# Attention and squared-ReLU feed-forward on one core: the order of issue planned from reads and writes

## The chip, the cores and the metric

The kernel runs on one core of one Trainium2 chip. The metric is the device time of one execution in microseconds (us). Three runs of the kernel before gave 759.31, 759.48 and 760.11 us; their median, 759.48 us, is the time before.

## The reference

There are B = 8 batches, H = 8 heads, S = 512 tokens, 32 state rows per head and D = 64. Both attentions below are computed, their results are joined, and every one of the 8 x (512 + 32) = 4608 rows goes through a feed-forward of width 2048.

```python
def _attn_ref(x, state):                        # x 8x8x512x64, state 8x8x32x64
    scores = scale * np.matmul(x, state.transpose(0, 1, 3, 2))
    a = softmax(scores)                         # over the 32 state rows
    xread = np.matmul(a, state)
    scores2 = scale * np.matmul(state, x.transpose(0, 1, 3, 2))
    a2 = softmax(scores2)                       # over the 512 tokens
    sread = np.matmul(a2, x)
    return np.concatenate([xread, sread], axis=2)

def _moe_ref(x, w_in, w_out):                   # w_in 512x2048, w_out 2048x512
    r = np.maximum(x @ w_in, 0.0)
    return (r * r) @ w_out
```

The weights arrive as 64-bit floats (looked at as pairs of 32-bit words) and are turned into 32-bit floats on the chip.

## The kernel before, in words

**Precision.** Products that need 32-bit accuracy at a high rate are made of three: a value is split into a rounded part `hi` and a remainder `lo` (`split`, L97: ScalarE copies, VectorE or GpSimd subtracts), and hi*hi, lo*hi and hi*lo are added up in PSUM.

**The main loop.** The token rows never form `xread`. Instead z = state x w_in is computed once per batch group, and the hidden layer of a batch is softmax x z. One *unit* is one batch b and one block `fc` of 128 hidden columns (16 units per batch, 128 in all). In `mlp` (L342) `up` makes 6 matmuls of 128x512 into `ph` (L353), then ScalarE takes the ReLU `r` (L355), VectorE multiplies `ph` by `r` (L359; for the first 10 units ScalarE squares, L357), and `split` gives `g_hi` and `g_lo` (L98, L99). `down` makes 12 matmuls of 128x512 into four accumulators `po` (L379), 8 of them with `g_hi` and 4 with `g_lo`. The up of a unit stands ahead of the down of earlier ones. The state rows of all batches (256) go through a last round of 16 units at the end, with 12 up matmuls of 128x256 and 6 down matmuls each.

**z.** `z_state` loads the states of four batches, `z_part` (L142) multiplies them by w_in: four matmuls over 64 rows, in two pairs (`pz0` on the upper 64 rows, `pz1` on the lower; L151), into two tiles, which ScalarE copies (L157) and a DMA writes to memory (`zd`). `z_fetch` (L179) reads a batch's share back in four DMAs (`z_raw`) and splits it. The group of batches 0 to 3 and that of 4 to 7 have 16 such parts each. For batch 0 the first three pairs of blocks are computed directly instead (`z_direct`, L165: `pzd`).

**The attention of a batch** is in two halves g of 256 channels. `scores` (L241) multiplies x by the states (`pst`, L257; from batch 2 on in split form, `pq`, L247). VectorE turns the result in blocks of 32 (`q`, L262), takes maxima and sums, subtracts and scales (L274 to L284), turns back (`at`, L286), and `split` gives `a_hi` and `a_lo`, without which no unit of the batch can start. In the first batches the subtraction and the scaling run on GpSimd (`pool_early`). `turn` and `read` (L297, L312: `pt`, `pr`) make the other attention two batches later.

**The weights.** Each of 16 tiles of w_in (256 columns of half the rows) and 16 of w_out is loaded (512 KB), converted by one ScalarE and three VectorE instructions (`singles`, L101: L104, L105, L108, L112), and w_out is also split, its `lo` on GpSimd (L412). All of it happens during batch 0. Four raw buffers hold tiles that are loaded and not yet converted.

**What sets the order.** The source lists the first steps by hand (L499) and spreads the rest over slots between ups and downs by due times (`Ahead`, L436). The tile framework then reorders all instructions by a timeline simulation of its own (`schedule_with_timeline_sim=True`, L639). Every engine takes its instructions in the order that results; nearly all loads are issued from one queue, SP's.

Of the kernel before, what the change touches and what calls it, by code (L numbers as in the profile page):

```python
# [9 lines left out]
F32 = mybir.dt.float32  # L10
# [6 lines left out]

@with_exitstack
def memory_attention_then_relu2_ffn(
# [10 lines left out]

# [10 lines left out]
    NCC = DM // P  # L52
    NFC = DF // P
# [27 lines left out]

    ident = const.tile([P, P], F32, name="ident")
    make_identity(nc, ident)

    wo = [None] * NFCH
    sp_hl = const.tile([P, NG, 2, 2, 2 * N], F32R, name="sp_hl")
    nc.gpsimd.memset(sp_hl.bitcast(F32), 0.0)
    sp_f = const.tile([P, NG, 2, P + D], F32, name="sp_f")
    nc.gpsimd.memset(sp_f, 0.0)
    sr = [const.tile([P, C], F32, name=f"sr{i}") for i in range(NGB)]  # L90
    wi = const.tile([P, NFCH, NCC, FW], F32, name="wi")
    zd, st = {}, {}
    for G in range(NGB):
        for k in range(NFCH):
            zd[G, k] = dr.tile([P, NG, HG, FW], F32, name=f"zd_{G}_{k}")

    def split(hi, lo, src, eng_lo):  # L97
        nc.scalar.copy(out=hi, in_=src)  # L98
        eng_lo.tensor_sub(out=lo, in0=src, in1=hi.bitcast(F32))  # L99

    def singles(out_f, words):  # L101
        low, high = words[..., 0], words[..., 1]
        bits = out_f.bitcast(I32)
        nc.scalar.activation(out_f, high.bitcast(F32), AF.Abs, scale=GUARD)  # L104
        nc.vector.tensor_scalar(  # L105
            out=bits, in0=bits, scalar1=3, scalar2=None, op0=ALU.logical_shift_left
        )
        nc.vector.scalar_tensor_tensor(  # L108
            out=bits, in0=high, scalar=-0x80000000, in1=bits,
            op0=ALU.bitwise_and, op1=ALU.bitwise_or,  # L110
        )
        nc.vector.scalar_tensor_tensor(  # L112
            out=bits, in0=low, scalar=29, in1=bits,
            op0=ALU.logical_shift_right, op1=ALU.bitwise_or,
        )
# [12 lines left out]
    def z_load(k, g):
        box = {}
        nq = NCC // NG  # L130

        def load():
            raw = sb.tile([P, nq, FW, 2], I32, name="w_raw", tag="raw", bufs=RAW)
            nc.sync.dma_start(out=raw.rearrange("p c f w -> p (c f w)"), in_=w_in[k * NG + g])
            box["raw"] = raw

        def convert():
            singles(wi[:, k, g * nq:(g + 1) * nq, :], box.pop("raw"))

        return load, convert  # L140

    def z_part(G, k, g):  # L142
        nq = NCC // NG

        def product():
            pz = [ps_x.tile([P, nq, FW], F32, name=f"pz{i}", tag="px") for i in range(2)]
            for q in range(nq):
                for i in range(2):
                    own = slice(i * D, (i + 1) * D)
                    cc = g * nq + q  # L150
                    nc.tensor.matmul(  # L151
                        pz[i][:, q, :], lhsT=st[G][own, cc, :], rhs=wi[own, k, cc, :],
                        start=True, stop=True,
                    )
            stage = sb.tile([P, nq, 2, FW], F32, name="z_stage", bufs=2)
            for i in range(2):
                nc.scalar.copy(out=stage[:, :, i, :], in_=pz[i])  # L157
            nc.scalar.dma_start(
                out=zd[G, k][:, g].rearrange("p h f -> p (h f)"),
                in_=stage.rearrange("p q i f -> p (q i f)"),  # L160
            )

        return product

    def z_direct(k, pool, tag):  # L165
        pz = pool.tile([P, NG, FW], F32, name="pzd", tag=tag)
        nq = NCC // NG
        for g in range(NG):
            for q in range(nq):
                nc.tensor.matmul(  # L170
                    pz[:, g, :], lhsT=sp_f[:, g].rearrange("p q n -> p (q n)")[:, q * P:(q + 1) * P],
                    rhs=wi[:, k, g * nq + q, :], start=q == 0, stop=q == nq - 1,
                )
        hi = sb.tile([P, NG, FW], F32R, name="z_hi", bufs=2)
        lo = sb.tile([P, NG, FW], F32R, name="z_lo", bufs=2)
        split(hi, lo, pz, nc.vector)
        return hi, lo

    def z_fetch(b, k):  # L179
        hi = sb.tile([P, NG, FW], F32R, name="z_hi", bufs=2)  # L180
# [4 lines left out]
        for j in range(HG):  # L185
            nc.sync.dma_start(out=raw[j * N:(j + 1) * N], in_=src[:, :, j, :])
# [456 lines left out]
```

## Time and profile before

| what | value |
|---|---|
| time, median of three runs | 759.48 us |
| time of the profiled execution | 758.9 us |
| its span, first to last instruction | 757.1 us |
| TensorE (PE) busy | 720.4 us, 3136 records |
| VectorE (DVE) busy | 437.4 us |
| ScalarE (ACT) busy | 379.7 us |
| GpSimd (POOL) busy | 154.3 us |
| mean granted TensorE clock | 0.96 |

PE busy is the union of modelled, overlapping matmul records; how much work stands in a stretch is seen from the distance of starts, not from it. PEld is the loading of weights. The granted clock is the share of full speed that TensorE was given. A matmul with plain 32-bit operands (`pst`, `pzd`, `pz`) leaves two records, one with split operands leaves one. The span is 1.8 us shorter than the execution's time.

### The profile page before, as it was taken

The page shows a single profiled execution, that of the slowest core. Times are in us where ns is not written, and L with a number is a line of the kernel's source. Part 1 is how long each engine was busy: PE and PEld are TensorE (multiplying, and loading weights), DVE is VectorE, ACT ScalarE, POOL GpSimd, SP SyncE. Part 2 cuts the span into 40 slices and gives each one's busy share as a digit, 9 for nine tenths or more (in the row PEclk, how much of TensorE's full clock was granted, in tenths as well). Part 3 has the DMA queues.
Part 4 walks back from the last instruction along what each step waited for, and adds up shares of the span by engine and source line. Part 5 has one row for each costly group of instructions (what it writes and reads, how often), then busy time and mean ns, then how long its engine had stood idle before and what let it go on. Part 6 is the DMA issues. An engine that isn't in the chain of part 4 may idle for free.

```text
span 757.1 us, 9414 instructions
## 1 busy us (share of the span) xinstructions
PE 720.4 (95%) x3136; PEld 562.1 (74%) x3136; DVE 437.4 (58%) x725; ACT 379.7 (50%) x714; POOL 154.3 (20%) x170
## 2 busy tenths in 40 slices
PE   4899799999999999986999999999999999999997
PEld 2566456778777776755888888888888888888896
DVE  5999952354854333356477487478468534534453
ACT  4477565354654443454465565466446534533443
POOL 1333540022410211023223222223213211100000
PEclk9589879999999999996999999999999999999999
DMA  9588632332123223242121321141213211200101
GB/s 303 199 276 281 239 143 90 111 122 87 58 86 127 102 92 111 99 180 82 45 86 60 118 78 57 57 139 58 62 61 117 80 28 47 66 28 1 57 1 28
DMA packets 49216, 76.90 MB, mean 102 GB/s; under 512 B 6800, under 2 KB 32528, under 8 KB 49168
## 3 DMA queue, kind: packets, MB, share of 16 engines
q1 hardware_dynamic: 44368, 59.27, 24.7%
q10 hardware_dynamic: 4800, 17.04, 5.6%
q8 instruction: 24, 0.39, 0.2%
q14 instruction: 24, 0.20, 0.1%
HBM read 50.59 MB, written 25.69 MB: 101 GB/s over the span
## 4 chain that ended last, share of the span: by engine, by line
PE 83%; DVE 7%; DMA 5%; ACT 2%; issue 1%; POOL 1%; SPq 1%; DVEq 0%; ACTq 0%
PE po L379 48%; PE ph L353 25%; PE pz L151 5%; PE pr L316 2%; DMA wo_raw<-w_out 2%; PE pq L247 1%; DVE wi L108 1%; DMA w_raw<-w_in 1%; DVE wof L108 1%; PE pt L304 1%; DVE wi L112 1%; DVE wof L112 1%; DMA xn_raw<-xn 1%; DVE wof L105 1%; DMA zd<-z_stage 1%
## 5 line engine op out<-in xcount | busy, mean ns | idle before, releaser
L379 PE MATMUL po<-wo_hi,g_hi 128*128 128x512 f32 x544 | 218.0, 401 | 3.2 <-ACT g_hi L98 3.2
L379 PE MATMUL po<-wo_lo,g_hi 128*128 128x512 f32 x544 | 214.9, 395 | 0.0
L359 DVE TENSOR_TENSOR ph<-ph,r 128x512 f32<-128x512 f32 (+1 forms) x134 | 89.1, 665 | 183.8 <-ACT r L355 183.4
L355 ACT ACTIVATE r<-ph 128x512 f32<-128x512 f32 (+1 forms) x144 | 82.7, 575 | 173.7 <-PE ph L353 173.2
L379 PE MATMUL po<-wo_hi,g_lo 128*128 128x512 f32 x544 | 152.1, 393 | 0.0
L99 DVE TENSOR_TENSOR g_lo<-ph,g_hi 128x512 fp32r<-128x512 f32 (+1 forms) x144 | 94.6, 658 | 58.5 <-ACT g_hi L98 34.2
L379 PEld LDWEIGHTS po<-wo_hi,g_hi 128*128 128x128 f32 x544 | 102.9, 189 | 29.7 <-ACT g_hi L98 5.6
L379 PEld LDWEIGHTS po<-wo_lo,g_hi 128*128 128x128 f32 x544 | 102.9, 189 | 23.0 <-issue 1.9
L379 PEld LDWEIGHTS po<-wo_hi,g_lo 128*128 128x128 f32 x544 | 101.0, 188 | 22.3 <-issue 1.0
L98 ACT CAST g_hi<-ph 128x512 fp32r<-128x512 f32 (+1 forms) x144 | 81.2, 564 | 48.5 <-DVE ph L359 36.9
L99 POOL TENSOR_TENSOR xn_hl<-xn_raw,xn_hl 128x512 fp32r<-128x512 f32 x32 | 42.7, 1335 | 230.8 <-ACT xn_hl L98 230.8
L353 PE MATMUL ph<-a_hi,z_hi 128*128 128x512 f32 x256 | 84.1, 410 | 1.2 <-ACT a_hi L98 0.7
L353 PE MATMUL ph<-a_hi,z_lo 128*128 128x512 f32 x256 | 84.6, 408 | 0.0
L353 PE MATMUL ph<-a_lo,z_hi 128*128 128x512 f32 x256 | 82.1, 402 | 0.0
L151 PE MATMUL pz<-wi,st_z 64*128 64x256 f32 x256 | 72.5, 443 | 9.4 <-ACT z_stage L157 5.6
L151 PEld LDWEIGHTS pz<-wi,st_z 64*128 64x128 f32 x256 | 43.1, 207 | 36.3 <-issue 9.8
L99 POOL TENSOR_TENSOR xt_hl<-xt_raw,xt_hl 128x512 fp32r<-128x512 f32 x24 | 31.4, 1309 | 151.9 <-ACT xt_hl L98 121.7
L353 PEld LDWEIGHTS ph<-a_hi,z_lo 128*128 128x128 f32 x256 | 49.5, 194 | 14.1 <-issue 2.6
L353 PEld LDWEIGHTS ph<-a_hi,z_hi 128*128 128x128 f32 x256 | 47.7, 193 | 15.4 <-issue 3.0
L157 ACT COPY z_stage<-pz 128x512 f32<-128x512 f32 x64 | 37.2, 588 | 43.3 <-PE pz L151 42.0
L353 PEld LDWEIGHTS ph<-a_lo,z_hi 128*128 128x128 f32 x256 | 49.5, 194 | 11.4 <-DVE wof L105 0.3
L99 DVE TENSOR_TENSOR z_lo<-z_raw,z_hi 128x512 fp32r<-128x512 f32 x61 | 45.1, 739 | 7.7 <-ACT z_hi L98 7.7
(116 smaller groups left out, 707.0 us busy)
## 6 DMA issues: line engine op xcount, KB each, us to landing
zd<-z_stage ACTq DMA_DIRECT2D x32, 512.0 KB, 2.8
z_raw<-zd SPq DMA_DIRECT2D x244, 64.0 KB, 2.3
xt_raw<-xT SPq DMA_DIRECT2D x16, 512.0 KB, 3.5
w_raw<-w_in SPq DMA_DIRECT2D x16, 512.0 KB, 5.0
wo_raw<-w_out SPq DMA_DIRECT2D x16, 512.0 KB, 4.3
xn_raw<-xn SPq DMA_DIRECT2D x16, 512.0 KB, 3.7
st_z<-stT SPq DMA_DIRECT2D x4, 128.0 KB, 5.9
sp_raw<-stP SPq DMA_DIRECT2D x7, 64.0 KB, 2.6
```

The costliest lines, as they stand in the source:

```text
L98: nc.scalar.copy(out=hi, in_=src)
L99: eng_lo.tensor_sub(out=lo, in0=src, in1=hi.bitcast(F32))
L105: nc.vector.tensor_scalar(out=bits, in0=bits, scalar1=3, scalar2=None, op0=ALU.logical_shift_left)
L108: nc.vector.scalar_tensor_tensor(out=bits, in0=high, scalar=-0x80000000, in1=bits, op0=ALU.bitwise_and, op1=ALU.bitwise_or,)
L112: nc.vector.scalar_tensor_tensor(out=bits, in0=low, scalar=29, in1=bits, op0=ALU.logical_shift_right, op1=ALU.bitwise_or,)
L151: nc.tensor.matmul(pz[i][:, q, :], lhsT=st[G][own, cc, :], rhs=wi[own, k, cc, :], start=True, stop=True,)
L157: nc.scalar.copy(out=stage[:, :, i, :], in_=pz[i])
L316: nc.tensor.matmul(pr[:, q].rearrange("p i c -> p (i c)"), lhsT=my["e"][:, t, q].rearrange("p i n -> p (i n)"), rhs=my["xn"][q][:, t].rear ...
L353: nc.tensor.matmul(ph, lhsT=w, rhs=v, start=i == 0, stop=i == len(todo) - 1)
L355: nc.scalar.activation(r, ph, AF.Relu)
L359: nc.vector.tensor_mul(out=ph, in0=ph, in1=r)
L379: nc.tensor.matmul(po[t], lhsT=g, rhs=w, start=i == 0 and j == 0, stop=i == last and j == 2)
```

## The change

A planner in the source takes the place of the hand-made list, of the slots and of the framework's reordering. Every step becomes an operation with its engines, a cost per engine, what it reads and writes, and sometimes a due time, an earliest time or a chain. `Planner.run` walks through time: at each step it takes the engine that can begin first and on it, of the operations that can begin within 0.02 us, the one due soonest; buffers are taken and given back as it goes. The order in which it picks is the program's order (`manual_schedule`, `schedule_with_timeline_sim=False`).

```diff
+class Planner:
+    RATE = 360.0
+    LAND = 2.2
...
+            t, e, o = best
...
+            o.run(e)
+            end = t + cost
+            if e == "POOL":
+                pool_end = end
+            elif o.both and e == "DVE":
+                end = max(end, pool_end + cost)
...
+def dve(n):
+    return ("DVE", 0.07 + n / 960)
...
+def gps(n):
+    return ("POOL", 0.15 + n / 450)
...
+    START, FIRST, STEP = 18.0, 5.4, 4.4
```

Besides the order, the work itself changes in these places.

**w_in by column tile.** A tile is now 128 columns of all 512 rows, so that one tile is what a unit needs; its size, its DMA and its conversion are as before. `z_direct` works on one block (6 calls of half the width), and `wi` is laid out by block.

```diff
-            np.ascontiguousarray(moe_w_in).view(np.int64).reshape(2, -1, 128, DF // 256, 256)
-            .transpose(3, 0, 2, 1, 4)
-        ).reshape(DF // 256 * 2, 128, -1),
+            np.ascontiguousarray(moe_w_in).view(np.int64).reshape(-1, 128, DF // 128, 128)
+            .transpose(2, 1, 0, 3)
+        ).reshape(DF // 128, 128, -1),
```

**Batch 0's softmax with tokens on partitions.** For batch 0 the scores are also computed turned (`sT`: 8 matmuls of 128x64 per half, with x as the weights), the softmax reads them from PSUM, and TensorE turns the result back (`pa`) in place of VectorE's two transposes. The untransposed product `pst`, which the other attention needs, is made later. Batch 0's subtraction and scaling run on VectorE, and so does the `lo` of w_out; from batch 2 on those of the softmax, with the `lo` of its result, run on GpSimd.

```diff
+            def product_t(e):
+                for t in range(NT):
+                    for q in range(NQ):
+                        nc.tensor.matmul(
+                            flat(sT.t)[:, t * P + q * 2 * N:t * P + (q + 1) * 2 * N],
+                            lhsT=xt.t[:, q, t * P:(t + 1) * P], rhs=sp_f[:, g, q, :2 * N],
+                            start=True, stop=True,
+                        )
...
+            begin=0.0 if b else START + 4.0,
...
-        split(wo[k][0][:, i, :], wo[k][1][:, i, :], wf, nc.gpsimd)
+        split(
+            lambda: wo[k][0][:, i, :], lambda: wo[k][1][:, i, :], lambda: wf.t, DM,
+            [wf], [("wo", 0, fc)], [("wo", 1, fc)],
+        )
```

**Down in pieces.** The 12 down matmuls of a unit are an operation of 8 (with `g_hi`) and one of 4 (with `g_lo`); in a batch's first unit the 8 are four operations of 2, in its last unit there are four of 3, one for each `po`, at the turn from one batch to the next. The four matmuls of a z part are one operation.

**What stands where now.** First, TensorE in the program's first rows. Before, the scores of batch 0 (`pst`) come first, then direct z (`pzd`), and a z part already stands ahead of and between the first unit's up (`ph`):

```order
L257 MATMUL pst<-xt_raw,sp_f 128x512 x4
L170 MATMUL pzd<-wi,sp_f 128x256 x10
L151 MATMUL pz_334<-wi,st_z 128x256 x2
L170 MATMUL pzd<-wi,sp_f 128x256 x2
L151 MATMUL pz_335<-wi,st_z 128x256 x2
L353 MATMUL ph<-a_hi,z_hi 128x512 x3
```

After, the turned scores come first, and only two blocks of direct z and the turning back stand ahead of the first up; `pst` comes behind two units' ups:

```order
L514 MATMUL sT<-sp_f,xt_raw 128x64 x16
L387 MATMUL pzd<-wi,sp_f 128x128 x4
L557 MATMUL pa<-ident,q_157 128x128 x4
L557 MATMUL pa<-ident,q_168 128x128 x4
L387 MATMUL pzd<-wi,sp_f 128x128 x4
L678 MATMUL ph<-a_hi,z_hi 128x512 x2
```

The first up moved ahead of two thirds of the direct z and of all z parts. Second, a z part of the second group on TensorE, in the middle of batch 2. Before, the framework put the pair of `pz0` (`pz_2131`) and that of `pz1` (`pz_2132`) at different places, here with half a down and half an up between:

```order
L151 MATMUL pz_2131<-wi,st_z 128x256 x2
L379 MATMUL po_1948<-wo_lo_574,g_hi 128x512
L379 MATMUL po_1949<-wo_hi_573,g_hi 128x512
L379 MATMUL po_1949<-wo_lo_574,g_hi 128x512
L379 MATMUL po_1946<-wo_hi_573,g_lo 128x512
L379 MATMUL po_1947<-wo_hi_573,g_lo 128x512
L379 MATMUL po_1948<-wo_hi_573,g_lo 128x512
L379 MATMUL po_1949<-wo_hi_573,g_lo 128x512
L353 MATMUL ph<-a_hi,z_hi 128x512 x2
L353 MATMUL ph<-a_hi,z_lo 128x512
L151 MATMUL pz_2132<-wi,st_z 128x256 x2
```

After, in batch 3, the four stand together and alternate between the two tiles, and an up stands between the 8 and the 4 matmuls of a down:

```order
L714 MATMUL po_2745<-wo_lo_87,g_hi 128x512
L678 MATMUL ph<-a_hi,z_hi 128x512 x2
L678 MATMUL ph<-a_hi,z_lo 128x512 x2
L678 MATMUL ph<-a_lo,z_hi 128x512 x2
L714 MATMUL po_2695<-wo_hi_86,g_lo 128x512
L714 MATMUL po_2703<-wo_hi_86,g_lo 128x512
L714 MATMUL po_2710<-wo_hi_86,g_lo 128x512
L714 MATMUL po_2745<-wo_hi_86,g_lo 128x512
L357 MATMUL pz_2912<-wi,st_z 128x256
L357 MATMUL pz_2913<-wi,st_z 128x256
L357 MATMUL pz_2912<-wi,st_z 128x256
L357 MATMUL pz_2913<-wi,st_z 128x256
```

All 32 z parts read like this now, and the up ahead of a unit's down is that of the unit three further on. Third, SP's queue during batch 0, where the loads of weights (`w_raw`, `wo_raw`) and of x (`xn_raw`) share the queue with what reads z back from memory (`z_raw` from `zd_3`, the first that batch 0 needs). Before, it stands behind every load of weights and two loads of x:

```order
L134 DMA w_raw<-w_in 128x1024
L405 DMA wo_raw<-w_out 128x1024 x3
L228 DMA xn_raw<-xn 128x4x256
L405 DMA wo_raw<-w_out 128x1024 x2
L228 DMA xn_raw<-xn 128x4x256
L186 DMA z_raw<-zd_3_87 32x2x256 x4
```

After, three such fetches stand among the loads of weights:

```order
L322 DMA z_raw<-zd_3_103 32x2x256 x4
L322 DMA w_raw<-w_in 128x1024 x2
L322 DMA wo_raw<-w_out 128x1024 x2
L322 DMA w_raw<-w_in 128x1024
L322 DMA z_raw<-zd_4_104 32x2x256 x4
L322 DMA w_raw<-w_in 128x1024
L322 DMA wo_raw<-w_out 128x1024 x2
L322 DMA w_raw<-w_in 128x1024 x2
L322 DMA wo_raw<-w_out 128x1024 x3
L322 DMA z_raw<-zd_5_105 32x2x256 x4
```

The reading back of z for batch 0's fourth pair of blocks (`zd_3`) moved from behind the loads of weights to a place ahead of the last 6 of w_in and 8 of w_out.

More of the change, by code (lines that the diff above doesn't have):

```diff
@@ L80, in memory_attention_then_relu2_ffn, with tile_ @@
     ps_x = ctx.enter_context(tc.tile_pool(name="ps_x", bufs=2, space=bass.MemoryType.PSUM))
+    BUFS = dict(
+        raw=4, xraw=2, x_hl=1, z_stage=2, st_z=1, z_raw=2, z_hi=2, z_lo=2, a_hi=2, a_lo=2,
+        sp_raw=2, st=1, at=1, st_low=1, q1=2, e2=4, s2=4, nm2=2, m1=2, s1=2, e_hl=1, both=1, low=1,
+        r=2, g_hi=2, g_lo=2, os_=3, wof=2, po=4, ph=2, px=2,
+    )
+    plan = Planner()
+    op = plan.op
+    def tile_(shape, dtype, name, tag=None):
+        tag = tag or name
+        pool = {"po": ps_o, "ph": ps_h, "px": ps_x}.get(tag, sb)
+        return Buf(pool, shape, dtype, name, tag, BUFS[tag], hot=tag in ("px", "x_hl"))
@@ L126, in z_state, with z_part, product @@
         st[G] = raw
[L128 to L147, printed above, removed]
+    def z_part(G, k, g, begin=0.0):
+        pz = [tile_([P, NQ, FW], F32, f"pz{i}", "px") for i in range(2)]
+        stage = tile_([P, NQ, 2, FW], F32, "z_stage")
+        def product(e):
+            for q in range(NQ):
@@ L156, in product @@
[L156 to L160, printed above, removed]
-            )
[L163 to L177, printed above, removed]
+        op(("PE", 1.2), product, r=[("wi", k * FPC + i) for i in range(FPC)] + [(st[G], 0), (st[G], 1)], w=pz, begin=begin)
@@ L179, in z_fetch @@
     def z_fetch(b, k):
-        hi = sb.tile([P, NG, FW], F32R, name="z_hi", bufs=2)
-        lo = sb.tile([P, NG, FW], F32R, name="z_lo", bufs=2)
-        raw = sb.tile([P, NG, FW], F32, name="z_raw", bufs=2)
+        raw = tile_([P, NG, FW], F32, "z_raw")
         at = (b % GB) * N
@@ L536, in aux @@
-    def aux():
-        weights.run()
-        reads.run()
-        slot[0] += 1
-    spill = {}
-    for b, fcs in parts:
-        zc = {}
-        while any(w["soft1b"] not in emitted for w in attentions[b][2]):
-            reads.next()
-        def first(fc, b=b, zc=zc):
-            k, i = divmod(fc, FPC)
-            if k not in zc:
-                zc[k] = direct.pop(k) if b == 0 and k < DIRECT else z_fetch(b, k)
-            f = slice(i * P, (i + 1) * P)
-            z_hi, z_lo = zc[k]
-            a_hi, a_lo = a_of[b]
+                        in0=both.t[i * N:(i + 1) * N, q, i * D:(i + 1) * D],
@@ L590, in first @@
[L590 to L603 removed]
+                (w.t[:, cc, :], v.t[:, cc, :])
@@ L605, in rows @@
             at = (t * GB + j) * R + S
-            eng = nc.sync if j % 2 else nc.scalar
-            eng.dma_start(out=out[at:at + N, :], in_=tile_[j * N:(j + 1) * N, :])
-    mlp(NS, range(NFC), first, rows, lambda: None)
+            load(
+                lambda at=at: out[at:at + N, :], lambda os_=os_, j=j: os_.t[j * N:(j + 1) * N, :], 64,
+                r=[os_], w=[("outs", t, j)], due=when[u] + 60, eng="SP" if j % 2 else "ACT", hold=None,
+            )
+    with tc.manual_schedule():
+        plan.run()
```

970 lines of the change are left out of this document (608 added, 362 removed).

## The prediction

> **What bounds the kernel now.** I read the page first, for the shares of the engines and TensorE's clock over time:
>
> ```profile
> PE 720.4 (95%) x3136; PEld 562.1 (74%) x3136; DVE 437.4 (58%) x725; ACT 379.7 (50%) x714; POOL 154.3 (20%) x170
> PEclk9589879999999999996999999999999999999999
> ```
>
> TensorE is the bound, and its clock drops in two places, in the first sixth and in slice 18 (about 340 us). What full speed means is read from the chain of waits in a quiet stretch:
>
> ```profile
> 668.79 2.75 PE po L379 x12
> 671.54 1.37 PE ph L353 x6
> 672.91 2.75 PE po L379 x12
> ```
>
> 18 matmuls of 128x512 take 4.12 us, 0.229 us each, and nothing else stands between. So a stretch loses time where its matmuls, at such prices, don't fill it. Then the windows, cut where the character changes:
>
> ```profile
> 0.00:33.00 33.00, 19.57 (x41) 10.74 (x42) 23.96 (x50) 14.63 (x28) 8.77 (x13) 0.82 0.77 253
> 33.00:61.00 28.00, 26.52 (x85) 18.10 (x86) 26.15 (x41) 20.07 (x37) 9.14 (x6) 0.79 0.80 260
> 61.00:81.00 20.00, 19.00 (x75) 13.27 (x75) 18.20 (x29) 12.75 (x24) 6.56 (x4) 1.00 0.89 295
> 81.00:107.00 26.00, 20.31 (x51) 11.57 (x51) 22.32 (x35) 15.67 (x32) 16.24 (x12) 0.67 0.51 181
> 107.00:161.00 54.00, 53.77 (x231) 39.79 (x228) 16.24 (x24) 23.70 (x43) 1.30 (x1) 1.00 0.31 110
> 161.00:330.00 169.00, 167.44 (x727) 126.98 (x725) 81.07 (x132) 82.31 (x152) 29.53 (x35) 1.00 0.28 96
> 330.00:356.00 26.00, 18.20 (x56) 12.39 (x56) 14.32 (x24) 14.81 (x30) 8.87 (x10) 0.67 0.42 156
> 356.00:705.00 349.00, 348.54 (x1579) 287.11 (x1580) 211.08 (x347) 174.95 (x326) 73.90 (x89) 1.00 0.21 66
> ```
>
> Columns: stretch, length, busy time and records of PE, PEld, DVE, ACT and POOL, granted clock, DMA share, GB/s. From 107 us on TensorE is busy throughout, except at 330 to 356. Up to 107 us only 252 matmul records start; DVE is busy for 90.6 of those 107 us and POOL for 40.7. The kernel is thus three things: a start bound by the conversion of weights and the first softmax, one hole at batch 3, and 570 us of pure TensorE.
>
> **The change, part by part.** *The first unit.* The timeline of the start:
>
> ```profile
> 2.26 1.36 SPq L200 DMA_DIRECT2D sp_f<-stP  x2
> 8.61 6.40 PE L257 MATMUL pst<-xt_raw,sp_f 128*128 128x512 f32 x8 [8.61 <-DMA sp_f<-stP]
> 14.85 1.89 PE L170 MATMUL pzd<-wi,sp_f 128*128 128x256 f32 x8
> 32.81 1.65 PE L353 MATMUL ph<-a_hi,z_hi 128*128 128x512 f32 x3
> ```
>
> TensorE waits for the states until 8.6 and for batch 0's `a_hi` until 32.8. After, the states are issued one load earlier: I take 8 us. No row shows the turned scores, 16 matmuls or 32 records of 64 columns. The nearest from below is `pzd` (0.236 us a record), from above the scores as they are (0.80 us a record of 512): 7.6 to 25.6 us. I take 7.6, since a record four times as narrow as `pzd` can at most be held by its weight load. The first half is then ready at 11.8 us and the second at 15.6. From there DVE's order holds 14 full-width operations and some small ones up to the second `a_lo`. What one costs is in the timeline:
>
> ```profile
> 23.48 0.43 DVE L105 TENSOR_SCALAR wi<-wi 128x512 int32<-128x512 int32 x1
> 23.81 0.69 DVE L112 SCALAR_TENSOR_TENSOR wi<-w_raw,wi 128x512 int32<-128x512 int32 x1
> 24.41 0.69 DVE L108 SCALAR_TENSOR_TENSOR wof<-wo_raw,wof 128x512 int32<-128x512 int32 x1
> 29.30 0.91 DVE L108 SCALAR_TENSOR_TENSOR wof<-wo_raw,wof 128x512 int32<-128x512 int32 x1
> 29.62 1.71 POOL L99 TENSOR_TENSOR wo_lo<-wof,wo_hi 128x512 fp32r<-128x512 f32 x1
> 30.13 1.48 DVE L105 TENSOR_SCALAR wi<-wi 128x512 int32<-128x512 int32 x1
> ```
>
> From start to start 0.33 us for a single-source operation, 0.60 for a two-source one; beside a POOL operation the same single-source one takes 1.48. 14 x 0.60 = 8.4 us of DVE work thus give the first up at 24 us (21 if the turned scores are faster, 28 with hand-overs), against 32.8.
>
> *The rest of batch 0.* After the change DVE's order holds, up to the 16th `g_lo`, 130 two-source operations, 36 single-source ones, 6 of half width and 18 small ones: 130 x 0.60 + 36 x 0.33 + 6 x 0.33 + 18 x 0.13 = 94 us. That includes the 16 `lo` of w_out that come from POOL; each costs DVE 0.60 us and frees it of a POOL operation like the one above, so it costs nothing or gains. Started at 12 us, DVE is done at 106 us. TensorE's order, from the first up to batch 0's last down, holds 300 matmuls of 128x512 (68.7 us; two of batch 1's ups among them), 15 z parts, `pst` and five of six direct blocks. The z parts:
>
> ```profile
> 50.83 1.13 PE L151 MATMUL pz<-wi,st_z 64*128 64x256 f32 x4
> 51.88 0.51 PE L379 MATMUL po<-wo_hi,g_hi 128*128 128x512 f32 x1
> 209.91 1.14 PE L151 MATMUL pz<-wi,st_z 64*128 64x256 f32 x8
> 210.98 0.51 PE L379 MATMUL po<-wo_hi,g_hi 128*128 128x512 f32 x1
> 72.26 1.88 PE L257 MATMUL pst<-xt_raw,sp_f 128*128 128x512 f32 x4
> 73.58 0.79 PE L379 MATMUL po<-wo_hi,g_hi 128*128 128x512 f32 x1
> ```
>
> A pair alone takes 1.05 us for 4 records; both pairs together take 1.07 for 8: the two halves of the rows work at the same time. So a z part that stands together costs 1.07 instead of 2.1. Hence 15 x 1.07 = 16.1; `pst` 4 x 1.32 = 5.3; direct blocks 40 records of half the width of `pzd`, 0.12 each, 4.8; transposes and reads 1.5. Together 96.4 us at full clock. To this come the clock and the pacing by DVE. In the first 33 us the clock is 0.82 and in the next 28 it is 0.79, about 12 us at half speed in each, most of it while TensorE hardly worked; I take 6 us lost (2 to 10). For pacing I take 5 (0 to 20): the up of the 11th unit needs a `z_lo` that stands behind 80 us of DVE work, 92 us, while TensorE reaches that up after 65 of its 96 us, 24 + 65 + 6 = 95; two engines that are level hold each other up a little. Batch 0's last down then ends at 24 + 96.4 + 11 = 131.4 us. Before:
>
> ```profile
> 160.24 0.85 PE L379 MATMUL po<-wo_hi,g_lo 128*128 128x512 f32 x3
> 94.04 22.85 SPq L186 DMA_DIRECT2D z_raw<-zd  x12
> 192.91 2.45 SPq L186 DMA_DIRECT2D z_raw<-zd  x4
> ```
>
> It ended at 161.1. The gain is 29.7 us.
>
> On the clock the Trainium skill ("TensorE: Matmul & The Clock Gate", Part 1) says that full speed returns after one busy window of about 3.4 us. By it only the first 3.4 us behind the first up are slow, 1.7 us lost instead of 6, and the sum would be 4 us lower. The rows above, a mean of 0.79 over 28 us in which TensorE was busy for 26.5, speak for more.
>
> *The z parts of the second group.* The windows, for the tile `pz` alone:
>
> ```profile
> 200.00:342.00 142.00, 32.17 (x128) 18.92 (x128) 18.44 (x32) 0.99 0.31 109
> ```
>
> All 16 parts of that group: 32.2 us of TensorE. After, 17 parts (one of the first group is left) at 1.07 are 18.2. TensorE is the bound here, so 14.0 us come off. This needs no good timing, only that the four stand together.
>
> *The hole at batch 3.* The timeline of TensorE:
>
> ```profile
> 344.19 1.19 PE L316 MATMUL pr<-xn_hl,e_hl 128*128 128x256 f32 x4 [2.42 <-DVE e_hl L99]
> 347.49 1.22 PE L316 MATMUL pr<-xn_hl,e_hl 128*128 128x256 f32 x4 [1.25 <-POOL xn_hl L99]
> 349.43 0.79 PE L353 MATMUL ph<-a_hi,z_hi 128*128 128x512 f32 x1 [0.72 <-ACT a_hi L98]
> 356.46 0.50 PE L379 MATMUL po<-wo_hi,g_hi 128*128 128x512 f32 x1 [1.54 <-ACT g_hi L98]
> ```
>
> Batch 2's downs were through, and batch 3's softmax was late: TensorE was left with the other attention's pieces, each behind DVE or POOL. The stretch 330 to 356 holds 18.2 us of work at clock 0.67, 12.2 at full clock: 13.8 us lost. After, the softmax of each batch is due with its first up and stands well ahead of it, and the second group's z parts are spread over batches 2 and 3, one between two units (the rows shown with the change). I count all 13.8 as gained; what is late next is the state rows' `read`, which nothing waits for until the tail.
>
> *Down in pieces and the turns.* The same matmuls; at the turn an accumulator comes free after 3 matmuls either way, and 348.54 of 349 us busy leave nothing to gain. Nothing. The tail has the same work and nearly the same order: nothing. The w_in tile is the same bytes in the same pieces: nothing by itself.
>
> **The sum.** Behind batch 0 the kernel before takes 757.1 - 161.1 = 596.0 us. Off come 14.0 and 13.8, and 1.9 for work done earlier (six ups, four reads at half a matmul's price). A fixed order that meets other times than planned adds small waits; 161 to 330 shows 1.6 of 169, so I add 3 (0 to 15). That is 569.3; with 131.4 the span is 700.7. The profiled execution took 758.9 us for its 757.1, and the median of the runs is 0.6 above it: 700.7 + 1.8 gives 702.5, and I say 702.
>
> **The rivals.** *SP's queue starves the start.* Three reads of z now stand ahead of loads of weights, and each waits there until its z part is computed, copied and written. The row above shows twelve such DMAs taking 22.85 us where 12 x 0.61 = 7.4 is their issue: 15.4 us of waiting. If the loads behind come that much late and DVE idles, batch 0 ends at 147 us: 718 us. Against it: four raw buffers are full ahead. A DVE that needs before's mean, (26.15 + 18.20 + 22.32) us over 105 operations or 0.635 each, would take 190 x 0.635 = 121 us instead of 94; the 11th up then comes some 20 us later, and batch 0 ends at about 150: 721 us.
>
> *The ups run too far ahead (slower).* In the steady part the up of a unit now stands between the downs of the one three before, and its `ph` is free only when the `g_lo` of the unit two before is made, which in turn waits for a down just ahead. Between that down and the up stand 8 matmuls, 1.83 us; the chain needs a finishing matmul (0.39 - 0.23), one `g_lo` (0.69) and two hand-overs, which I take as 0.1 each: 1.05. If DVE is late there by more than 0.7 us in every unit, TensorE waits in all 112 units behind batch 0; from 0.52 us each (58 us) on the change loses all it gains: 762 us. The row of the waits that bears on it (total, times, longest, in us):
>
> ```profile
> DVE g_lo L99 <- PE po L379: 21.7, 15, 2.7
> ```
>
> Before, `g_lo` waited so 15 times, and TensorE lost nothing by it (167.44 of 169). So this is unlikely.
>
> *Only the steady gains.* The start is paced as before by conversions and ends at 161: 702 + 30 = 732.
>
> **Chances.** Forecast 0.70 (its own range 688 to 716), SP or DVE pacing 0.13, only the steady gains 0.07, ups too far ahead 0.05, better than 688 0.05. About 0.2% is what a measurement of this kernel can tell from no change. All but the slower rival and a chance of 0.02 that many small waits eat the gain are faster. The low end: first up at 21, 2 lost to clock, none to pacing and none later, 702 - 3 - 4 - 5 - 3 = 687. The high end takes in both prices of the first rival (718 and 721) and 5 us of small waits on top: 726.
>
> **What would show it.** First up near 24 us; batch 0's last down near 131; `pz` groups of 8 records in 1.07 us throughout and about 18 us for the second group; no stretch with a clock below 0.9 after 60 us; gaps of under 0.2 us per unit behind batch 0. It is wrong if SP's `z_raw` shows waits of over 5 us with `w_raw` behind them, or if TensorE's idle time is put to `ph`'s release by `g_lo`.

## The result and the profile after

| | before | after |
|---|---|---|
| time, median | 759.39 us (758.84 to 760.11, 4 runs) | 703.76 us (702.46 to 706.06, 4 runs) |
| profiled execution, span | 758.9, 757.1 us | 703.2, 701.2 us |
| first up starts | 32.8 us | 23.7 us |
| batch 0's last down ends | 161.1 us | 140.5 us |
| behind it, to the span's end | 596.0 us | 560.7 us |

The ratio is 0.927, 95% interval 0.9244 to 0.9297: faster by 55.6 us, where 57 were forecast. The page of the kernel after, its busy times and TensorE's clock:

```profile
PE 676.6 (96%) x3200; PEld 546.7 (78%) x3200; DVE 367.9 (52%) x639; ACT 424.3 (61%) x803; POOL 148.7 (21%) x169
PEclk9999998999999999999999999999999999999999
```

The second drop of the clock, near 340 us, is gone, and of the first the page shows one slice; finer windows, further down, find three drops of 3 to 7 us. The windows of the kernel after, cut as those of before (length, then busy time and records of PE, PEld, DVE, ACT, POOL, then clock, DMA share, GB/s):

```profile
...
33.00:61.00 28.00, 27.50 (x146) 21.46 (x145) 25.64 (x54) 19.75 (x41) 0.00 (x0) 1.00 0.76 263
61.00:81.00 20.00, 16.79 (x68) 10.79 (x69) 16.00 (x30) 13.01 (x24) 0.00 (x0) 0.91 0.79 253
81.00:107.00 26.00, 20.91 (x91) 14.22 (x90) 22.58 (x42) 18.41 (x37) 3.71 (x3) 0.91 0.77 275
107.00:131.00 24.00, 23.64 (x108) 18.50 (x108) 18.80 (x30) 18.53 (x35) 9.08 (x9) 0.95 0.44 154
...
161.00:330.00 169.00, 169.00 (x782) 138.21 (x780) 92.45 (x162) 108.40 (x203) 57.43 (x60) 1.00 0.27 89
330.00:356.00 26.00, 26.00 (x128) 19.32 (x127) 7.61 (x13) 14.21 (x27) 0.00 (x0) 1.00 0.39 140
356.00:649.00 293.00, 293.00 (x1367) 240.16 (x1366) 136.72 (x225) 175.09 (x321) 72.37 (x83) 1.00 0.24 78
...
```

Two things are to be seen. From 161 to 649 us TensorE is never idle, at 330 to 356 neither: the hole is closed. And between 61 and 107 us it stands still for 8.3 of 46 us, while DVE is not full either (38.6 of 46 us): that is where batch 0 became later than forecast. The timeline of TensorE at the start and at those two stops (the bracket is the idle time before, and what ended it):

```profile
6.06 7.06 PE L514 MATMUL sT<-sp_f,xt_raw 128*128 128x64 f32 x32 [6.06 <-DMA sp_f<-stP]
...
23.67 1.20 PE L678 MATMUL ph<-a_hi,z_hi 128*128 128x512 f32 x2
...
26.51 1.54 PE L357 MATMUL pz<-wi,st_z 64*128 64x256 f32 x8
27.98 0.73 PE L678 MATMUL ph<-a_hi,z_hi 128*128 128x512 f32 x2
...
29.48 1.02 PE L464 MATMUL pst<-xt_raw,sp_f 128*128 128x512 f32 x2
...
66.93 0.73 PE L678 MATMUL ph<-a_hi,z_hi 128*128 128x512 f32 x2 [1.79 <-ACT z_hi L285]
...
103.67 2.56 PE L357 MATMUL pz<-wi,st_z 64*128 64x256 f32 x8 [3.33 <-ACT z_stage L365]
106.16 1.22 PE L678 MATMUL ph<-a_hi,z_hi 128*128 128x512 f32 x2
```

The up at 66.93 is the first that needs z read back from memory. The chain of waits behind it shows the writing of that z, SP's issue of the fetch, and weights that land late after it:

```profile
51.04 0.96 ACT z_stage L365 x2
...
52.03 8.63 DMA zd<-z_stage
...
60.68 0.61 SPq L322
...
64.22 4.54 DMA w_raw<-w_in
...
76.69 6.46 DMA w_raw<-w_in
```

What a z part costs now, in the timeline and, behind batch 0, in the windows for the tile `pz` alone:

```profile
140.39 1.13 PE L357 MATMUL pz<-wi,st_z 64*128 64x256 f32 x8
141.46 0.50 PE L714 MATMUL po<-wo_hi,g_hi 128*128 128x512 f32 x1
```

```profile
140.00:365.00 225.00, 12.48 (x88) 7.57 (x88) 11.82 (x22) 1.00 0.31 102
365.00:650.00 285.00, 6.81 (x48) 4.13 (x48) 6.55 (x12) 1.00 0.23 77
```

From start to the next start a part takes 1.07 us, all eight records together, and the 134 records that start behind batch 0's end take 17.8 us in all by that measure (31.8 for 128 before; all 17 parts, with two records that start just ahead of that end, take 18.1).

### The profile page after: what moved, and what is told of

It reads as the page before. It is cut to its first block, busy times and chain, and to the rows that moved or that the text cites. A ratio compares the mean times of both kernels' runs of the same rounds, so it can differ in the third digit from the quotient of the medians.

```text
span 701.2 us, 9451 instructions
## 1 busy us (share of the span) xinstructions
PE 676.6 (96%) x3200; PEld 546.7 (78%) x3200; DVE 367.9 (52%) x639; ACT 424.3 (61%) x803; POOL 148.7 (21%) x169
## 4 chain that ended last, share of the span: by engine, by line
PE 89%; DMA 4%; DVE 3%; ACT 2%; SPq 1%; issue 1%; POOL 0%; ACTq 0%; DVEq 0%; POOLq 0%
PE po L714 51%; PE ph L678 27%; PE pz L357 3%; PE pr L619 2%; PE pq L486 2%; DMA w_raw<-w_in 2%; DMA zd<-z_stage 1%; PE sT L514 1%; PE pzd L387 1%; PE pt L601 1%; SPq L322 1%; DMA z_raw<-zd 1%; DVE wi L308 1%; DVE wi L314 1%; DMA sp_f<-stP 0%
## 5 line engine op out<-in xcount | busy, mean ns | idle before, releaser
L288 DVE TENSOR_TENSOR g_lo<-ph,g_hi 128x512 fp32r<-128x512 f32 (+1 forms) x144 | 94.4, 656 | 154.9 <-PE po L714 123.2
L692 DVE TENSOR_TENSOR ph<-ph,r 128x512 f32<-128x512 f32 (+1 forms) x59 | 40.1, 680 | 126.1 <-ACT r L684 126.0
L678 PE MATMUL ph<-a_hi,z_hi 128*128 128x512 f32 x256 | 81.6, 400 | 1.9 <-ACT z_hi L285 1.8
L678 PE MATMUL ph<-a_hi,z_lo 128*128 128x512 f32 x256 | 80.4, 396 | 0.0
L288 POOL TENSOR_TENSOR xn_hl<-xn_raw,xn_hl 128x512 fp32r<-128x512 f32 x32 | 45.7, 1429 | 151.0 <-ACT xn_hl L285 113.8
L678 PEld LDWEIGHTS ph<-a_hi,z_lo 128*128 128x128 f32 x256 | 48.8, 191 | 11.2 <-DVE z_lo L288 0.8
L288 POOL TENSOR_TENSOR xt_hl<-xt_raw,xt_hl 128x512 fp32r<-128x512 f32 x24 | 33.0, 1374 | 109.8 <-ACT xt_hl L285 109.8
L288 DVE TENSOR_TENSOR z_lo<-z_raw,z_hi 128x512 fp32r<-128x512 f32 x61 | 47.0, 771 | 12.6 <-ACT z_hi L285 12.6
L690 ACT ACTIVATE ph<-r 128x512 f32<-128x512 f32 (+1 forms) x85 | 48.7, 572 | 2.0
L365 ACT COPY z_stage<-pz 128x512 f32<-128x512 f32 x64 | 34.7, 592 | 15.9 <-PE pz L357 14.7
L357 PE MATMUL pz<-wi,st_z 64*128 64x256 f32 x256 | 38.7, 414 | 4.3 <-ACT z_stage L365 3.3
```

The costliest lines, as they stand in the source:

```text
L288: lambda e: ENGINE[e].tensor_sub(out=lo(), in0=src(), in1=hi().bitcast(F32)),
L357: nc.tensor.matmul(pz[i].t[:, q, :], lhsT=st[G].t[own, cc, :], rhs=wi[own, k * FPC:(k + 1) * FPC, cc, :], start=True, stop=True,)
L365: act(512), lambda e, i=i: nc.scalar.copy(out=stage.t[:, :, i, :], in_=pz[i].t),
L678: nc.tensor.matmul(ph.t[:, :width], lhsT=w, rhs=v, start=j == 0, stop=j == len(pairs_) - 1)
L690: nc.scalar.activation(ph.t[:, :width], rl.t[:, :width], AF.Square)
L692: nc.vector.tensor_mul(out=ph.t[:, :width], in0=ph.t[:, :width], in1=rl.t[:, :width])
```

## The experiments

The theory was that the 55 us have three sources: z parts whose two pairs stand together, a softmax that no longer leaves a hole, and a start that begins earlier. What was open was the start, which came 9 us late. All times below are medians; the kernel before, run beside each, had 759.4 to 760.9 us, and the ratio is to it. The last two columns show where batch 0 and batch 2 end: the order is planned anew in each, so that work moves from one batch to another, and only at the second of them is about the same work done.

| kernel | time, us | ratio (95%) | first up | batch 0 ends | batch 2 ends |
|---|---|---|---|---|---|
| changed kernel | 703.76 | 0.927 (0.9244 to 0.9297) | 23.7 | 140.5 | 285.1 |
| the same, again | 702.51 | 0.9248 (0.9226 to 0.9269) | 23.5 | 139.4 | 284.0 |
| pairs apart | 750.72 | 0.9871 (0.9841 to 0.9901) | 23.0 | 156.7 | 307.6 |
| landing known | 708.92 | 0.931 (0.9283 to 0.9337) | 23.1 | 149.2 | 293.0 |
| softmax not turned | 712.69 | 0.9361 (0.9333 to 0.9389) | 27.3 | 143.5 | 289.5 |
| wo_lo on GpSimd | 705.40 | 0.9267 (0.9244 to 0.929) | 23.6 | 139.6 | 287.0 |
| 16 direct blocks | 702.55 | 0.9256 (0.9227 to 0.9284) | 23.6 | 117.4 | 284.1 |
| 10 direct blocks | 709.32 | 0.9327 (0.9288 to 0.9366) | 23.8 | 142.2 | 291.9 |
| three raw buffers | 711.01 | 0.9366 (0.9344 to 0.9389) | 19.8 | 152.9 | 295.6 |
| five raw buffers | 702.42 | 0.9231 (0.92 to 0.9263) | 23.6 | 134.6 | 286.6 |
| softmax on VectorE | 703.87 | 0.9273 (0.9244 to 0.9302) | 23.7 | 140.1 | 285.6 |
| fetches off SP | 705.39 | 0.9284 (0.9219 to 0.9349) | 24.2 | 139.2 | 287.0 |
| before, pairs together | 787.18 | 1.0354 (1.0304 to 1.0404) | 30.8 | 178.0 | 334.4 |

**The pairs apart.** Each z part is two operations, and the plan lets the second wait for the first's copy, so that other work comes between.

```diff
-        def product(e):
-            for q in range(NQ):
-                for i in range(2):
+        for i in range(2):
+            def product(e, i=i):
+                for q in range(NQ):
...
-        op(("PE", 1.2), product, r=[("wi", k * FPC + i) for i in range(FPC)] + [(st[G], 0), (st[G], 1)], w=pz, begin=begin)
+            op(
+                ("PE", 1.05), product,
+                r=[("wi", k * FPC + j) for j in range(FPC)] + [(st[G], i)] + ([(stage, 0)] if i else []),
+                w=[pz[i]], begin=begin,
+            )
```

> Only the z parts are undone: each is two operations again, and the planner puts other matmuls between the pair on the upper 64 rows and the pair on the lower. Theory (the pairs save time only where they stand together): a part costs 2 x 1.05 = 2.10 us instead of 1.06. Behind batch 0, where TensorE is the bound and 134 of the records stand, that is 134 / 8 x 1.04 = 17.4 us; in batch 0 another 15 x 1.04 = 15.6, of which an unknown share is hidden by the 20 us that TensorE waits there. 721 to 737 us, I take 726. Rival (the gain of 14 us behind batch 0 is one of order, and the pieces are no dearer apart): the z parts behind batch 0 stay near 18 us in all and the time within 3 us of 704.

It cost about 46 us, more than either theory said. TensorE's timeline, and `pz` behind batch 0:

```profile
313.50 1.13 PE L357 MATMUL pz<-wi,st_z 64*128 64x256 f32 x4
314.56 0.50 PE L717 MATMUL po<-wo_hi,g_hi 128*128 128x512 f32 x1
```

```profile
157.00:365.00 208.00, 13.54 (x52) 8.05 (x52) 7.53 (x13) 1.00 0.28 92
365.00:650.00 285.00, 22.63 (x88) 14.39 (x88) 12.80 (x22) 0.99 0.27 89
```

Half a part (4 records) now takes the 1.06 us that a whole one took. From start to start the records behind batch 0 (140, six more than in the changed kernel) take 35.7 us instead of 17.8, 17.9 more (17.4 expected), and those of batch 0 39.4 instead of 24.7. Batch 0 ends 16.2 us later, so nothing of its share was hidden, and by this measure 33 us are the pairs. Of the other 13 or so, 7 are TensorE standing still between 356 and 649 us, which the changed kernel never does there; the rest is put to no step:

```profile
356.00:649.00 293.00, 285.98 (x1279) 227.68 (x1278) 126.58 (x209) 172.05 (x316) 76.48 (x89) 0.99 0.26 88
```

Without the pairs the new order is only 1.3% faster than the kernel before. The three sources therefore do not simply add up: undoing this one takes back 46 of the 56 us.

**The pairs together in the kernel before.** The opposite edit, in the framework's own order:

```diff
-            for q in range(nq):
+            with tc.manual_schedule():
+                for q, f in [(0, 2)] + [(q, FW) for q in range(nq)]:
...
-                        pz[i][:, q, :], lhsT=st[G][own, cc, :], rhs=wi[own, k, cc, :],
+                            pz[i][:, q, :f], lhsT=st[G][own, cc, :], rhs=wi[own, k, cc, :f],
```

> The kernel before, with one thing of the change alone: the four matmuls of a z part stand together. Two matmuls of 2 columns ahead of them take both tiles first, and a region of fixed order holds the six; the framework still orders the rest by its own simulation. In all parts but one the four are adjacent in TensorE's order. Theory (the pairs save time where they stand together, whoever makes the order): the second group's parts take 17 to 18 us instead of 32.2, 14 us off, 2 to 4 us on for the 64 small matmuls, and a few us off or on in the start, 743 to 751 us. Rival (the order of the rest is what counts): 756 to 762 us.

Neither: it is 27 us slower than before. The timeline shows why it does not test the pairs cleanly:

```profile
209.57 0.38 PE L152 MATMUL pz<-wi,st_z 64*128 64x2 f32 x2
209.88 0.50 PE L380 MATMUL po<-wo_hi,g_hi 128*128 128x512 f32 x1
...
214.22 1.35 PE L152 MATMUL pz<-wi,st_z 64*128 64x2 f32 x10
215.50 0.50 PE L380 MATMUL po<-wo_hi,g_hi 128*128 128x512 f32 x1
```

The first small matmul stands alone and takes 0.31 us, then the rest 1.28: 0.5 us in such a part for the two small matmuls, where 0.1 was allowed (0.2 where all six stand together, 1.29 us), and one of the two `px` tiles is held for 4.65 us meanwhile. The other attention needs those tiles, and the hole at batch 3 grew:

```profile
330.00:384.00 54.00, 36.80 (x159) 25.43 (x158) 22.72 (x40) 24.76 (x49) 11.85 (x12) 0.73 0.37 137
```

So this run does not show what the pairs alone are worth in the old order. It shows that standing together has to be planned with the buffers.

**Softmax on VectorE.**

```diff
-        return [[dve(n)], [dve(n), gps(n)]][b] if b < 2 else [gps(n)]
+        return [dve(n)]
```

> The softmax's subtraction and scaling and the remainder of its result run on VectorE in all batches instead of on GpSimd from batch 2 on (and, in batch 1, on either); the planner orders anew. Theory (the hole at batch 3 closed because the order puts each batch's softmax ahead of the batch's first up): no hole, the stretch behind batch 0 stays at 560 to 563 us, 702 to 707 us in all. Rival (it closed because GpSimd took this work from VectorE): the hole or small waits return, 5 to 14 us, 709 to 718.

No difference, and no hole:

```profile
330.00:356.00 26.00, 26.00 (x128) 19.51 (x129) 7.47 (x13) 13.93 (x27) 0.00 (x0) 1.00 0.40 144
```

So it is not the engine that closed the hole. Nor is it the pairs: with the pairs apart TensorE is busy for 26.00 of these 26 us too. The order, with the softmax due ahead of its batch, is what remains; no run changes that alone.

**Softmax not turned.**

```diff
-        turned = b == 0
+        turned = False
...
-                begin=0.0 if b else START + 4.0,
+                begin=0.0,
```

> Batch 0's softmax as that of batch 1: no turned scores, two transposes on VectorE in their place; the planner orders anew. Theory (batch 0's end follows the first up): pst takes 6.4 us a half where sT takes 3.8, and two full-width VectorE operations per half are added, 4 x 0.60, so the first up comes 5 to 8 us later, at 29 to 32, and the time is 708 to 712. Rival (the start is paced by the conversion of weights, whatever the first up): first up as late, but batch 0 ends within 2 us of 140.5, 702 to 706 us.

The first up came 3.6 us later and batch 2's end 4.4: the end follows the first up, by less than expected. Behind batch 2 this kernel's span has another 4.4 us more (420.5 and 416.1), with TensorE full in both. That is neither theory's: it is the pace of the matmuls, in the chain of a quiet stretch of this kernel and of the changed one:

```profile
605.34 2.76 PE po L714 x12
608.11 1.39 PE ph L678 x6
```

```profile
601.77 2.72 PE po L714 x12
604.49 1.36 PE ph L678 x6
```

18 matmuls take 4.15 us here and 4.08 there, with nothing between them in either.

**The changed kernel again.** 

> The changed kernel itself, once more, beside the next three. Nothing is edited. 703 to 706 us. One number is looked at besides: TensorE's spacing of two down matmuls has the median 227 ns in the changed kernel and in three of the experiments so far, 231 ns in the kernel before and 232 in the one whose softmax is not turned. If that goes with the execution, it will differ here; if with the program, it will be 227 again.

702.51 us, and the median spacing is 227 ns again, as in all other kernels made from it but the one whose softmax is not turned. In the experiment made from the kernel before it is 231, as in that kernel. So the pace goes with the program, as far as one repeat can show it.

**The landing known to the planner.**

```diff
-                o.end = queue + self.LAND
+                o.end = queue + self.LAND + o.lat
...
-            r=[(stage, 0), (stage, 1)], w=[("zd", G, k, g)], eng="ACT", issue=0.35, hold=None,
+            r=[(stage, 0), (stage, 1)], w=[("zd", G, k, g)], eng="ACT", issue=0.35, hold=None,
+            lat=6.0,
```

> The planner is told that what z parts write lands 6 us later than it thought (8.2 instead of 2.2 us behind the copy), so the fetches that read it move to later places in SP's queue; nothing else is edited, though the rest of the order follows. Theory (batch 0 ended 9 us later than forecast because SP stands at a fetch whose data has not landed, with weight loads queued behind it): SP's wait at the first fetch shrinks below 1 us, the later weight loads come 3 us earlier, and batch 0's last down comes at 133 to 137 us instead of 140.5; 697 to 701 us. Rival (it is VectorE's pacing, or the landing itself that the units wait for): batch 0 ends at 140 or later, 702 to 708 us.

About 4 us slower. SP's wait at the first fetch, 5.5 us in the changed kernel, is gone, as the theory asked (from 54 to 64 us SP waits for no `zd`), and yet the 7th unit's up starts at 68.2 us instead of 66.9. The third fetch (`zd_5`) moved behind both loads of x, and the units that need it and the next ones came later: the 11th unit's up at 108.3 us instead of 106.2, the 15th's at 136.5 instead of 123.2. The theory's prediction failed.

**Fetches off SP.**

```diff
-                r=[("zd", b // GB, k, g) for g in range(NG)], w=[(raw, j)], issue=0.62, hold=30.0, chain="zf",
+                r=[("zd", b // GB, k, g) for g in range(NG)], w=[(raw, j)], issue=0.62, hold=30.0,
+                chain="zf", eng="SP" if b else "POOL",
```

> The changed kernel, with batch 0's fetches of z issued from GpSimd's queue instead of SP's; GpSimd is idle from 33 to 81 us. All loads of weights stay on SP's, in nearly the same order, with nothing between them that waits for a landing. Theory (SP standing at a fetch, with weight loads queued behind it, is what batch 0 lost 9 us by): batch 0's last down comes at 133 to 137 us instead of 140.5, 696 to 701 us. Rival (it is the landing of the written z itself, 5 to 9 us, and the reading back behind it, on whatever queue): batch 0 ends at 139 or later, 702 to 707 us.

Batch 0 ends 1.3 us earlier and the time is not shorter. From 30 to 107 us TensorE is busier here (first row) than in the changed kernel (second), but behind that, at 113.56 us, it stops for 3.27 us before a `pr` of the other attention:

```profile
30.00:107.00 77.00, 72.22 (x335) 50.97 (x334) 68.69 (x134) 58.43 (x115) 12.40 (x20) 0.98 0.79 278
```

```profile
30.00:107.00 77.00, 68.20 (x310) 47.79 (x309) 66.62 (x128) 54.17 (x107) 3.71 (x3) 0.95 0.76 261
```

So up to 4 us may be the queue's, but the order was planned anew too, and the kernel does not keep them. The chain of this kernel where the first fetch stands:

```profile
52.67 7.86 DMA zd<-z_stage
...
60.83 1.76 POOL z_raw L322 x3
62.59 5.72 DMA z_raw<-zd
...
68.41 0.63 ACT z_hi L285
```

With nothing of it in SP's queue, the way of z through memory still takes 7.86 + 5.72 us. From the first fetch's issue to `z_hi` it is 7.6 us here (60.83 to 68.41) and 5.6 in the changed kernel (60.68 to 66.3). It is the landing that the unit waits for. The Trainium skill ("Trainium Kernel Development and Optimization", Key Constraints) says that DMAs from SP, ScalarE and GpSimd share the same 16 engines, so that another queue saves only the time of issue. This case agrees: the four fetches were issued in 2.3 us instead of 3.4, and the data came no sooner.

**Direct blocks.**

```diff
-    DIRECT = 6
+    DIRECT = 16
```

> All 16 blocks of batch 0's z are computed directly (before: 6), so batch 0 reads nothing back and no fetch of z stands among the weight loads; all 32 z parts stay, since batches 1 to 7 need them. TensorE gets 10 more direct blocks, 10 x 0.89 = 8.9 us of work. Theory A (batch 0 is late because of the writing and reading back of z and of SP standing in it): most of the 20 us that TensorE lost in batch 0 come back, 10 to 15 of them, so the time is 697 to 703 us although there is more work. Theory B (it is the loads of weights and their conversion, with or without the fetches): TensorE loses the 20 us again, the extra work comes on top, 710 to 715 us.

The windows of this kernel show TensorE nearly full where it stood before, at clock 1.00:

```profile
33.00:61.00 28.00, 27.72 (x144) 22.91 (x144) 26.80 (x55) 20.35 (x40) 0.00 (x0) 1.00 0.75 249
61.00:81.00 20.00, 19.82 (x103) 16.52 (x102) 19.84 (x41) 13.01 (x24) 0.00 (x0) 1.00 0.56 194
81.00:107.00 26.00, 25.93 (x131) 19.77 (x130) 21.91 (x43) 15.54 (x30) 0.00 (x0) 1.00 0.39 142
```

8.3 us of idle TensorE came back between 33 and 107 us, and 8.9 us of work were paid for it. The later drops of the clock are gone as well, which by the figures below is worth about 4 us more; batch 2 ends only 1.0 us earlier, and the time is the same. So theory A is right that the stops come with the writing and reading back of z, which this edit takes away together with SP's standing at it, and the cure is worth nothing. With 10 blocks (`DIRECT = 10`):

> As the experiment with 16 direct blocks, with 10: 4 more than in the changed kernel, 4 x 0.89 = 3.6 us of work more on TensorE. The first fetch of z then stands behind all but five of the weight loads. Theory (what 16 blocks brought, 9 us, comes mostly from taking the first fetches out of the weight loads): 6 to 9 us less are lost for 3.6 of work, 697 to 701 us. Rival (each block brings what it costs): 702 to 705 us.

It is slower by about 5 us. In its trace the up of the 14th unit starts at 103.7 us and that of the 15th at 127.8: in the new order the last fetch of batch 0 stands behind the loads of x. Both theories missed.

**Raw buffers.** Three in place of four, then five (with two output buffers in place of three, for room):

```diff
-        raw=4, xraw=2, x_hl=1, z_stage=2, st_z=1, z_raw=2, z_hi=2, z_lo=2, a_hi=2, a_lo=2,
+        raw=3, xraw=2, x_hl=1, z_stage=2, st_z=1, z_raw=2, z_hi=2, z_lo=2, a_hi=2, a_lo=2,
```

> Three buffers for loaded and not yet converted weights in place of four; the planner orders anew. Theory B (batch 0 is paced by the landing of weight loads, 4 to 6 us each, issued only when a buffer is free): a quarter less in flight costs VectorE several waits more, batch 0's last down 4 to 12 us later, 708 to 716 us. Theory A (the reading back of z paces it): within 2 us of the changed kernel, 702 to 707.

> Five buffers for loaded and not yet converted weights in place of four; their room comes from the output staging, two buffers in place of three, used only at the turns of batches. The planner orders anew. Theory (batch 0 is paced by how many weight loads are under way, each 4 to 9 us from issue to landing; three buffers cost 8.5 us): batch 0's last down 3 to 6 us earlier, at 134 to 138, and 696 to 701 us. Rival (the DMA engines, busy for 0.77 of the stretch from 33 to 107 us, or the order itself set the pace, and a fifth buffer only makes loads queue longer): 702 to 708 us.

With three, the first up is 3.9 us earlier, but batch 0 ends 12.4 us later and the time rises by about 8. With five it ends 5.9 us earlier, as the theory said, and the time stays: batch 2 ends no sooner. What batch 0 gained, batch 1 gave back: one up and one z part stand behind batch 0 instead of in it, and TensorE stops for 3.0 us behind it, where the changed kernel is full:

```profile
131.00:165.00 34.00, 31.00 (x149) 23.34 (x146) 21.70 (x38) 23.35 (x48) 10.83 (x12) 1.00 0.37 134
```

Fewer loads under way cost; more do not help.

**wo_lo on GpSimd.**

```diff
-            [wf], [("wo", 0, fc)], [("wo", 1, fc)],
+            [wf], [("wo", 0, fc)], [("wo", 1, fc)], engs=[gps(DM)],
```

> The 16 remainders of w_out (wo_lo) go back to GpSimd, as before the change; the planner orders anew. Theory (VectorE and GpSimd hinder each other): VectorE is freed of 16 x 0.60 = 9.6 us, but each GpSimd operation of 1.5 to 1.8 us holds up the VectorE operations beside it by about 1 us, 16 us, so batch 0 ends 2 to 8 us later, 706 to 712. Rival (the work counts where it is done): VectorE is done 9.6 us sooner and batch 0 ends 3 to 6 us earlier, 698 to 701.

705.4 us and the same ratio: neither slower nor faster, and between what the two theories gave. The first 107 us of this kernel and of the changed one, in the windows:

```profile
0.00:107.00 107.00, 87.47 (x379) 64.35 (x380) 86.56 (x153) 68.41 (x130) 28.21 (x26) 0.95 0.71 252
```

```profile
0.00:107.00 107.00, 87.31 (x386) 64.02 (x387) 83.03 (x160) 65.24 (x125) 5.56 (x11) 0.96 0.70 240
```

VectorE has 7 operations fewer there and is busy for 3.5 us more. A mean over all would mix different operations; shape by shape it is the conversions that take longer. The costliest of them in these 107 us, here and in the changed kernel:

```profile
L308 DVE SCALAR_TENSOR_TENSOR wi<-w_raw,wi 128x512 int32<-128x512 int32 x16 | 15.0, 953 | 0.0
```

```profile
L308 DVE SCALAR_TENSOR_TENSOR wi<-w_raw,wi 128x512 int32<-128x512 int32 x16 | 10.8, 683 | 0.0
```

That is 4.3 us for this group, and some 9 for all six groups of conversions. The 14 `wo_lo` that VectorE makes in these 107 us of the changed kernel, at 0.683 us each, are 9.6. So the slowing that the theory named is there, and it eats what the moved work frees.

## Why the prediction was right, and where it was not

*The first up.* 24 us forecast, 23.67 measured. The turned scores take 7.06 us for 32 records, 0.221 each (0.236 taken); the states came at 6.1 us (8 taken), and DVE's order and hand-overs took the rest: 10.6 us from the last score to the first up, where 14 x 0.60 = 8.4 were counted. The start that came early and the stretch that took longer cancel, so the nearness is partly luck.

*The rest of batch 0.* This is the step that failed: 131.4 us forecast, 140.5 measured. From the first up to the last down there are 116.8 us for the 96.4 us of work, 20.4 lost where 11 were allowed. The clock term held. The windows that hold the two later drops:

```profile
68.00:72.00 4.00, 4.00 (x12) 2.71 (x12) 3.18 (x6) 3.22 (x7) 0.00 (x0) 0.57 0.74 280
102.00:109.00 7.00, 5.33 (x15) 3.97 (x16) 5.15 (x13) 4.49 (x9) 1.91 (x2) 0.53 0.91 300
```

Behind the first up TensorE was slow for about 3.8 us (by the rows above, six matmuls in 2.84 us from 23.67 on, six in 1.50 from 27.98 on). In the two windows the missing share of the clock, 0.43 of 4 us and 0.47 of the 5.3 that are busy, is 1.7 and 2.5 us: about 1.9 + 1.7 + 2.5 = 6.1 us, with 6 forecast. It was put together wrongly, though: not one long slow start, but a short one and two more at the stops of 1.79 and 3.33 us. At half speed the three lasted about 3.8, 3.4 (0.43 of 4) and 6.6 us (0.47 of 7, in which TensorE was idle for 1.7). The rule of the Trainium skill that the prediction weighed ("TensorE: Matmul & The Clock Gate", Part 1), full speed after a busy window of about 3.4 us, fits the first two, and the third is about two such windows, the first of them not busy throughout; the mean of before that I took, some 12 us at half speed, fits none.

What was mis-sized is "for pacing I take 5": it was 14 (20.4 less the 6.1). By the windows 9 of these are stops of TensorE from 33 to 131 us; the other 5 are put to no step. I had asked when DVE would be done with its work; what the 7th unit waited for was z on its way through memory, 8.63 us of writing and the fetch behind it. The longest stop, 3.33 us at 103.67, belongs to the writing too: that z part waits for ScalarE's copy into `z_stage`, which had itself waited 1.06 us for an earlier `zd` to be written.

Two of my own signs of being wrong came: the clock fell below 0.9 twice after 60 us, and SP stood at a fetch for over 5 us with loads of weights behind it (30 to 107 us; total, times, longest):

```profile
SPq L322 <- DMA zd<-z_stage: 7.8, 3, 5.5
```

Batch 0 nevertheless ended at 140.5 us, between my 131 and that rival's 147. VectorE's mean was 0.519 us (83.03 over 160 operations in the first 107 us), so the rival's second price, at 0.635, did not arise. The ground of the first rival was there, then, but SP's standing was not what the time hung on: with the landing known to the planner the wait at the first fetch went and batch 0 ended later, with the fetches off SP it ended 1.3 us earlier. And the runs with 16 direct blocks and with five buffers show that removing the wait does not shorten the kernel by itself.

*The z parts.* 14.0 us forecast behind batch 0, 14.0 measured (31.8 - 17.8; 13.7 with all 17 parts). The run with the pairs apart shows cause and size.

*The hole and the small waits.* Behind batch 0, 569.3 us were forecast and 560.7 measured. From start to start, the sums by product from batch 0's last down to the last of the tail:

| | ph | po | pq | pr | pt | pz | sum |
|---|---|---|---|---|---|---|---|
| before | 179.2 | 334.8 | 14.0 | 20.0 | 10.7 | 31.8 | 590.5 |
| after | 172.6 | 333.9 | 11.2 | 14.1 | 6.0 | 17.8 | 555.6 |

The 21 us outside `pz` are the hole, the waits around the other attention, work done earlier (five `ph`, some 1 us) and the pace. The 3 us added for small waits did not come: 169.00 of 169 and 293.00 of 293 us busy. The pace of the matmuls gives about 3 us more (mean spacing of neighbours 230.2 ns before, 228.8 after, some 2300 matmuls), which no term had. About 2.5 us are put to no step. The two misses, 9.1 us late and 8.6 early, cancel; the total is nearer than its parts.

*The rivals.* Ups too far ahead: refuted by the busy shares, though the waits of the row shown for it have grown:

```profile
DVE g_lo L288 <- PE po L714: 123.2, 53, 4.7
```

DVE waits 123 us in all for downs, before it can make `g_lo`; yet TensorE never waits for that `ph`, since DVE's 0.7 us fit into the 8 matmuls between. Only the steady gains: refuted by the first up and batch 0's end.

*What stays open.* What sets the pace of the first 165 us. Four ways of relieving it (GpSimd's help, fetches elsewhere, no fetches, five buffers) moved the time by under 3 us, two other orders cost 4 to 7. VectorE is busy there for 83 of the first 107 us and the DMA engines for about three quarters of 33 to 107 us; no run lightened both. Whether the pace of the matmuls comes from where the program's tiles lie was not tried. No version beat the changed kernel by more than the intervals can tell.

## What to carry to other kernels

Matmuls over different halves of the rows are worth twice as much when they stand together and alternate, and a scheduler that moves single instructions can lose that without any wait showing in the profile: compare the time of a group from start to start with that of the same group elsewhere. A data path through memory has a landing time at both ends, and when the end of one stage moves earlier, look one or two stages on before counting it, since work that was moved out of it is still to be done.

## What was not expected of the hardware

- The spacing of neighbouring 128x512 matmuls went with the program: median 227 ns in the changed kernel and all its relatives but one, 231 in the kernel before and its relative, 232 with the softmax not turned. Behind batch 2 the last made 4.4 of 416 us, about 1%.
- TensorE fell to half speed for 3.4 us after a stop of 1.79 us (66.93 us) in the start; after stops of 1.42 and 1.18 us (74.24 and 88.68 us) it did not (clock 1.00 from 72 to 102 us).
- A 64-row matmul of two columns standing alone between 128-row ones takes 0.31 us, nearly a third of a whole z part.
